# Gate and up as seven products of halves, positions in another order, joins by accumulating transfers, operands at multiples of 256 bytes

## The chip, the cores and the metric

The kernel runs on one core of one Trainium2 chip. The metric is the device time of one execution in microseconds (us). TensorE (PE; its weight loads are PEld), VectorE (DVE), ScalarE (ACT), GpSimd (POOL) and SyncE (SP) each work through their own instructions in order and wait for each other by semaphores. SyncE issues the transfers between main memory and the on-chip memory; a transfer that adds to its target is issued by GpSimd.

## What is computed

Position count S is 2,048, width D 640, hidden width F 1,536, 32 heads of 20 features. With x the input and xn its layer norm:

```python
qkv = xn @ wqkv                       # 640 -> 3 x 640
logits = q . k[i - 2w], w = 0..7      # each position sees itself and every second one before it
o = softmax(logits * scale) . v
s = o @ wo
h = (xn @ w_gate) * (xn @ w_up)       # 640 -> 1536, no nonlinearity
g = silu(h @ w_down)                  # 1536 -> 640
out = x + s * g
```

Since each position attends at distance 2, the even and the odd positions never meet: they are two independent rows.

## The kernel before, in words

All matrix products are done in three parts to keep float32's precision: each operand is split into hi (rounded to float32r, a ScalarE cast, L85) and lo (the rest, a subtraction, L86), and hi x hi, hi x lo and lo x hi are added in PSUM (`ALL3`, `mm3` at L95, `qkv` at L295).

The positions form 16 tiles of 128, `s` 0 to 7 even and 8 to 15 odd, in 4 chunks of 512 columns (`CH`). The even tiles are normalised and transposed on TensorE (`trans`, L229 to L231), the odd ones on VectorE (`trans_odd`, L209, L256, L259, L261); hi and lo of all four chunks then stay on chip in tiles `xc`.

Attention is split into 6 groups of heads (5 or 6 heads, 300 or 360 columns of q, k and v) and two halves of positions: 12 units (`UN`), ordered group by group, even then odd. For a unit TensorE does 8 x 15 products (`qkv`, L295), ScalarE takes q and k, v out of PSUM (L297, L298), a transfer shifts k and v by one partition (kv<-kv), and VectorE does the attention: 4 products with k (L329) each reduced (L332), the softmax (L336 to L345, with ScalarE's exponential at L341), 4 products with v (L350), 3 sums (L358) and a last one (L361). The result is stored in `o_scr`.

Between units TensorE does pieces of gate and up: for each of 12 blocks `f` of 128 hidden features and each of 4 chunks, 15 products of 512 columns for gate and 15 for up. ScalarE copies gate out (`gs`, L397), VectorE multiplies it by up (`hs`, L408; before the attention starts and after it ends, ScalarE and GpSimd do this at L410 and L411), and a transfer stores it in `h_scr` (L412). The weights of a block are loaded into `wraw`, cast by ScalarE and subtracted by GpSimd (`split_wf`).

The code is emitted in the order in which it shall run on each engine. VectorE's attention is a generator: `advance(budget)` gives it the TensorE time that has just been emitted, times `PACE`, as credit, and each of its steps costs an estimate in us; `finish_piece` places the multiplications, and `drain(u - 2)` ends a unit's attention before the unit after next begins. After the last block come the output projection (`out_proj`, tiles 0 to 15, 30 products of 320 columns each, L95; its operand is transposed by `trans_o`, L467, L85, L86), meanwhile the weights of down are summed and split, and at last down as seven products of halves for each pair of tiles (`product`, L606, 56 x 18 products), with silu (L587) and the gating (L592, L593).

The tiles' places in the on-chip memory follow from the order of their allocation. `xc` and `wf` begin at 128 or 96 bytes past a multiple of 256, and the qkv weights have rows of 1,200 or 1,440 bytes.

## Time and profile before

| | |
|---|---|
| runs shown | 787.12, 787.69, 788.05 us; median 787.69 |
| profiled execution, first to last instruction (span) | 786.0 us |
| around the span, by the median | 1.7 us |
| TensorE, VectorE, ScalarE, GpSimd busy | 778.0, 659.3, 234.2, 147.9 us |
| products on TensorE | 4,454 |
| moved by transfers | 92.7 MB, 118 GB/s in the mean |

All times within the profile count from the first instruction. "Busy" is the time in which an engine executes anything; a product's record reaches into the next one, so that the distance from product to product is read from a run of them (15 products in 3.50 us), not from a record. A line such as L95 is a line of the kernel before.

### The profile page before, as it was taken

The numbers are of one execution on the slowest core, as the hardware profiler recorded it, in microseconds if no ns is written. First come the engines' busy times: TensorE is split into PE (matmuls) and PEld (weight loads), VectorE is DVE, ScalarE is ACT, GpSimd is POOL, SyncE is SP. The second block draws the span as 40 slices with busy tenths as digits, with TensorE's granted clock in tenths as the row PEclk, the third lists the DMA queues.
The fourth block names the chain that finished last, engine by engine and source line by source line (L and its number), as shares of the span: only waits on it lengthen the run. The fifth ranks groups of instructions, "written<-read, shape, count | busy, mean of one in ns | idle before, by whom it ended". The sixth has DMA issues, their size and how long they took to land.

```text
span 786.0 us, 11222 instructions
## 1 busy us (share of the span) xinstructions
PE 778.0 (99%) x4454; PEld 708.9 (90%) x4454; DVE 659.3 (84%) x660; ACT 234.2 (30%) x536; POOL 147.9 (19%) x110
## 2 busy tenths in 40 slices
PE   8999999999999999999999999999999999999997
PEld 6889898888898898899898989888899999999997
DVE  6889899999999979996999999992177667777775
ACT  5334211121112111311221202012366564444442
POOL 5301211022013200410231000112467600000000
PEclk9999999999999999999999999999999999999999
DMA  8172122141132321404033131332797574555534
GB/s 321 67 230 75 42 61 72 48 123 48 50 83 89 95 71 61 117 28 112 28 105 86 58 86 58 107 103 66 160 274 209 170 270 131 206 200 188 182 101 135
DMA packets 81661, 92.68 MB, mean 118 GB/s; under 512 B 23032, under 2 KB 63304, under 8 KB 81480
## 3 DMA queue, kind: packets, MB, share of 16 engines
q1 hardware_dynamic: 81608, 91.96, 38.2%
q8 instruction: 35, 0.57, 0.3%
q14 instruction: 18, 0.15, 0.1%
HBM read 54.53 MB, written 28.31 MB: 105 GB/s over the span
## 4 chain that ended last, share of the span: by engine, by line
PE 97%; DMA 2%; ACT 1%; DVE 0%; SPq 0%; POOL 0%; issue 0%
PE q L295 26%; PE u L95 21%; PE g L95 21%; PE q L606 11%; PE q L95 9%; PE u L606 5%; PE g L606 3%; DMA wraw<-in_wgu 1%; DMA wraw<-in_wqkv 1%; PE q L229 0%; ACT wf L85 0%; SPq L135 0%; ACT wqh L85 0%; ACT xc L230 0%; POOL wql L86 0%; PE q L249 0%
## 5 line engine op out<-in xcount | busy, mean ns | idle before, releaser
L95 PE MATMUL u<-xc,wf 128*128 128x512 f32 (+1 forms) x735 | 176.2, 390 | 0.0
L95 PE MATMUL g<-xc,wf 128*128 128x512 f32 (+1 forms) x735 | 176.1, 390 | 0.0
L95 PEld LDWEIGHTS u<-xc,wf 128*128 128x128 f32 x735 | 135.7, 187 | 32.2
L95 PEld LDWEIGHTS g<-xc,wf 128*128 128x128 f32 x735 | 135.3, 187 | 31.0
L295 PE MATMUL q<-wqh,xc 128*128 128x300 f32 (+1 forms) x960 | 159.8, 309 | 2.1 <-DVE xc L231 1.2
L295 PEld LDWEIGHTS q<-wqh,xc 128*128 128x128 f32 x960 | 146.0, 188 | 4.3 <-DVE xc L231 1.5
L329 DVE TENSOR_TENSOR t<-q,kv 128x1600 f32<-128x1600 f32 (+1 forms) x48 | 97.9, 2040 | 10.1 <-DMA kv<-kv 10.1
L350 DVE TENSOR_TENSOR t<-e,kv 128x1600 f32<-128x1600 f32 (+1 forms) x48 | 97.5, 2051 | 1.1
L86 POOL TENSOR_TENSOR wf<-wraw,wf 128x256 fp32r<-128x256 f32 (+2 forms) x22 | 48.8, 2232 | 248.1 <-ACT wf L85 248.1
L332 DVE TENSOR_REDUCE lg<-t 128x80 f32<-128x1600 f32 (+1 forms) x48 | 92.6, 1930 | 1.2
L397 ACT ACTIVATE gs<-g 128x512 f32<-128x512 f32 x48 | 28.7, 598 | 205.9 <-PE g L95 197.2
L295 PE MATMUL q<-wql,xc 128*128 128x300 f32 (+1 forms) x480 | 86.3, 309 | 0.0
L358 DVE TENSOR_TENSOR t<-t,t 128x1600 f32<-128x1600 f32 (+1 forms) x36 | 80.2, 2228 | 1.1
L295 PEld LDWEIGHTS q<-wql,xc 128*128 128x128 f32 x480 | 74.4, 188 | 0.0
L297 ACT ACTIVATE kv<-q 128x200 f32<-128x200 f32 (+1 forms) x96 | 33.4, 348 | 129.4 <-PE q L295 129.4
L606 PE MATMUL q<-xc,wf 128*128 128x320 f32 x432 | 67.3, 309 | 0.0
L606 PEld LDWEIGHTS q<-xc,wf 128*128 128x128 f32 x432 | 64.3, 188 | 0.0
L86 POOL TENSOR_TENSOR wql<-wraw,wqh 128x300 fp32r<-128x300 f32 (+4 forms) x15 | 34.0, 2292 | 142.7 <-ACT wqh L85 142.7
L95 PE MATMUL q<-wf,wf 128*128 128x320 f32 x156 | 35.7, 310 | 0.0
L408 DVE TENSOR_TENSOR hs<-u,gs 128x512 f32<-128x512 f32 x39 | 26.6, 683 | 0.6 <-issue 0.6
L95 PEld LDWEIGHTS q<-wf,wf 128*128 128x128 f32 x156 | 26.1, 188 | 0.0
L86 DVE TENSOR_TENSOR wf<-ot,wf 128x640 fp32r<-128x640 f32 x13 | 15.5, 1190 | 11.9 <-ACT wf L85 11.9
(161 smaller groups left out, 888.9 us busy)
## 6 DMA issues: line engine op xcount, KB each, us to landing
h_scr<-hs SPq DMA_DIRECT2D x48, 256.0 KB, 2.3
wraw<-in_wgu SPq DMA_DIRECT2D x12, 640.0 KB, 4.9
t<-h_scr SPq DMA_DIRECT2D x8, 768.0 KB, 7.8
hs<-s_scr SPq DMA_DIRECT2D x16, 320.0 KB, 4.0
gs<-in_x SPq DMA_DIRECT2D x16, 320.0 KB, 4.4
wraw<-h_scr SPq DMA_DIRECT2D x12, 384.0 KB, 5.9
out<-q SPq DMA_DIRECT2D x14, 320.0 KB, 3.7
wraw<-in_wd SPq DMA_DIRECT2D x12, 320.0 KB, 4.8
```

Of the source, the lines that this page charges most:

```text
L86: eng.tensor_sub(lo, raw, hi.bitcast(F32))
L95: nc.tensor.matmul(acc, a, b, start=first and n == 0, stop=last and n == len(runs) - 1)
L295: nc.tensor.matmul(p, xT[(r * NE + i) // TPC][a][:, k, t0:t0 + P], wq[g][b][:, k], start=n == 0, stop=n == len(runs) - 1, skip_group_check ...
L297: nc.scalar.activation(kv_t[u][:, :, W - 1 + i, :], p[:, c:].rearrange("p (a c) -> p a c", a=2), AF.Copy)
L329: nc.vector.tensor_mul(t, q.rearrange("p i c -> p (i c)").unsqueeze(1).to_broadcast([P, 2, NE * c]), places(0, j))
L332: nc.vector.tensor_reduce(out=lg[:, :, j:j + 2].rearrange("p n a -> p a n"), in_=heads(t), op=ALU.add, axis=AX.X)
L350: nc.vector.tensor_mul(heads(t), pw, heads(places(1, j)))
L358: nc.vector.tensor_add(acc, acc, t)
L397: nc.scalar.activation(gs, pp[0], AF.Copy)
L408: nc.vector.tensor_mul(hs, pp[1], gs)
L606: nc.tensor.matmul(p, y[:, i, k], wd_t[name][k][:, l], start=new and r == 0, stop=r == len(runs) - 1, skip_group_check=True)
```

## The change

- **Seven products.** For 17 pairs of a block of hidden features and a half of the positions (`JOBS` of kind "S"), gate and up of both chunks are computed together: the two chunks are one side's halves, gate and up the other's, and the 640 contracted features are two halves of 256 and a rest of 128. Seven products on sums of weight blocks and sums of x blocks (`strassen`, L628) give the four results in 54 products of 512 columns; the rest of 128 is added into the same PSUM tiles. Seven other pairs (kind "P") stay as they were, 60 products. The last of the seven products of a job is deferred (`flush`) behind the first two of the next job or into the next unit.
- **Joins.** ScalarE copies the products out of PSUM, three accumulating transfers of 256 KB issued by GpSimd add them up (L656, L665, L669), and VectorE multiplies the joined results (L680).
- **Sums of weights and of x.** GpSimd forms four sums of each S block (L179 to L182), stored in `w_scr` and loaded again for the odd half. VectorE forms 9 sums of x for each half of the positions (L335 to L352), ScalarE and GpSimd split them.
- **Lo parts of weights.** Instead of a subtraction ScalarE writes the negative of hi into lo, and an accumulating transfer adds the weights from main memory (L154, L203 to L206).
- **Order.** All six groups of the even positions come first, then the six of the odd ones; the qkv weights are loaded for each unit, 12 times. Transposed tiles are stored in `xt_scr` (by way of the two buffers `ot`); hi and lo of the odd chunks are made later from it, and only one half's x stays on chip beside its sums. `ORDER` sets the sequence of jobs and units, `later` the emission of preparations some us of estimated TensorE time after their load, and `PACE` is 0.95.
- **Places.** Two unused tiles and padded rows put both operands of every large product at multiples of 256 bytes.

```diff
-PACE = 1.0
+PACE = 0.95
+MM = 0.2135
+GATE, UP = (0, 1, 2, 3, 6), (8, 9, 4, 5, 7)
+W_ROWS = ((0, 0), (1, 0), (2, 0), (3, 0), (2, 1), (3, 1), (4, 0), (4, 1), (0, 1), (1, 1))
...
+    ORDER = ("P", "S", "U", "S", "S", "U", "S", "S", "U", "S", "S", "U", "P", "P", "U", "P", "P", "U",
+             "S", "S", "U", "S", "S", "U", "S", "S", "U", "S", "S", "U", "S", "S")
+    JOBS = [(f, 0, "P" if f in (0, 1, 2, 10, 11) else "S") for f in range(KF)]
+    JOBS += [(f, 1, "P" if f in (10, 11) else "S") for f in (10, 11, 3, 4, 5, 6, 7, 8, 9, 0, 1, 2)]
+    FEED = {i: ((i + 2, 0),) for i in range(len(JOBS) - 2) if i not in (10, 11)}
+
+    def end_job(i):
+        for j, d in FEED.get(i, ()):
+            load_wf(j)
+        if i == len(JOBS) - 2:
+            load_wo(0)
+            load_wo(1)
+            later(7, lambda: (split_wo(0), split_wo(1)))
...
+    def later(us, act):
+        events.append((clock[0] + us, len(events), act))
+        events.sort(key=lambda e: e[:2])
+
+    def step(us):
+        clock[0] += us
+        while events and events[0][0] <= clock[0]:
+            events.pop(0)[2]()
+        advance(PACE * us)
...
+        cp = -(-c3 // 64) * 64
+        raw = st([P, KD, cp], "wql", 1)[:, :, :c3]
+        for k0, k1 in ((0, 3), (3, KD)):
+            nc.sync.dma_start(raw[:, k0:k1], wqkv[g][:, k0:k1])
+        later(7, lambda: split_wq(u, raw))
+
+    def split_wq(u, raw):
+        g = UN[u][0]
+        c3 = raw.shape[2]
+        cp = -(-c3 // 64) * 64
+        hi = st([P, KD, cp], "wqh", 1, F32R)[:, :, :c3]
+        ks = ((0, 2), (2, 4), (4, KD))
+        for k0, k1 in ks:
+            nc.scalar.activation(hi[:, k0:k1], raw[:, k0:k1], AF.Copy)
+        lo = st([P, KD, cp], "wql", 1, F32R)[:, :, :c3]
+        for k0, k1 in ks:
+            negate(hi[:, k0:k1], lo[:, k0:k1])
+        nc.gpsimd.dma_start(lo, wqkv[g], accum_op=ALU.add)
+        wq[u] = hi, lo
...
+    def wf_tile(dt=F32R):
+        return st([P, 16, P], "wf", 4, dt)
+
+    def load_wf(i):
+        f, r, kind = JOBS[i]
+        raw = wf_tile(F32)
+        if kind == "P":
+            nc.sync.dma_start(raw[:, :10], wgu[f])
+            later(6, lambda: split_wf(i, raw))
+        elif r and (f, 0, "S") in JOBS:
+            nc.sync.dma_start(raw[:, :8], wgu[f, :, :8])
+            nc.sync.dma_start(raw[:, 8:], w_scr[f])
+            later(7, lambda: split_wf(i, raw))
+        else:
+            nc.sync.dma_start(raw[:, :8], wgu[f, :, :8])
+            a21 = st([P, 2, P], "ot", 2)
+            nc.sync.dma_start(a21, wgu[f, :, 8:])
+            later(6, lambda: sum_wf(i, raw, a21))
+
+    def sum_wf(i, a, a21):
+        nc.gpsimd.tensor_add(a[:, 8:10], a21, a[:, 4:6])
+        nc.gpsimd.tensor_sub(a[:, 12:14], a[:, 0:2], a21)
+        nc.gpsimd.tensor_sub(a[:, 10:12], a[:, 8:10], a[:, 0:2])
+        nc.gpsimd.tensor_sub(a[:, 14:16], a[:, 2:4], a[:, 10:12])
+
+        def store():
+            nc.sync.dma_start(w_scr[JOBS[i][0]], a[:, 8:])
+            split_wf(i, a)
+
+        later(4, store)
...
+        def low():
+            lo = wf_tile()
+            for k0, k1 in cuts:
+                negate(hi[:, k0:k1], lo[:, k0:k1])
+            if kind == "P":
+                nc.gpsimd.dma_start(lo[:, :10], wgu[f], accum_op=ALU.add)
+            else:
+                nc.gpsimd.dma_start(lo[:, :8], wgu[f, :, :8], accum_op=ALU.add)
+                nc.gpsimd.dma_start(lo[:, 8:], w_scr[f], accum_op=ALU.add)
+            set_wf(i, hi, lo)
+
+        later(2.5, low)
...
+    st([P, 32], "skip", 1)
...
+    def store_xT(s, y):
+        c = (s % TPC) * P
+        nc.sync.dma_start(xt_scr[s // TPC, :, :, c:c + P], y)
...
+    def load_xS(r):
+
+        (ah, al), (bh, bl) = [[x_tile(1 - r), x_tile(1 - r)] for _ in range(2)]
+        a, b = xt_scr[2 * r], xt_scr[2 * r + 1]
+        xS[r] = {"T1": (ah, al, 0), "T2": (ah, al, 2), "T3": (bh, bl, 0), "T4": (bh, bl, 2), "D5": (ah, al, 4)}
+
+        def block(k):
+            ta, tb = st([P, 2, CH], "wraw", 3), st([P, 2, CH], "wraw", 3)
+            nc.sync.dma_start(ta, a[:, k:k + 3:2])
+            nc.sync.dma_start(tb, b[:, k:k + 3:2])
+
+            def sums():
+                nc.vector.tensor_sub(ta[:, 0], tb[:, 0], ta[:, 0])
+                nc.vector.tensor_sub(tb[:, 0], tb[:, 1], tb[:, 0])
+                nc.vector.tensor_sub(tb[:, 1], tb[:, 1], ta[:, 0])
+                nc.vector.tensor_sub(ta[:, 1], ta[:, 1], tb[:, 1])
+                credit[0] -= 2.4
+
+            later(8, sums)
+            for n, (t, hi, lo, j) in enumerate(((ta[:, 0], ah, al, k), (tb[:, 0], bh, bl, k),
+                                                (tb[:, 1], ah, al, k + 2), (ta[:, 1], bh, bl, k + 2))):
+                later(11 + 1.5 * n, lambda t=t, hi=hi, lo=lo, j=j: parts(nc.gpsimd, t, hi[:, j], lo[:, j]))
...
+            if k0 == 0:
+                full = st([P, KD, P], "ot", 2)
+            nc.scalar.activation(full[:, k0:k1], p, AF.Copy)
...
+        store_xT(s, full)
...
-        hi, lo = xT_tile(s)
-        nc.scalar.activation(hi, y, AF.Copy)
-        low_parts()
-        halves.append(lambda: nc.vector.tensor_sub(lo, y, hi.bitcast(F32)))
...
+        store_xT(s, y)
...
+    st([P, 24], "gap", 1)
...
-            if running:
-                nc.vector.tensor_mul(hs, pp[1], gs)
-            else:
-                nc.scalar.activation(hs, pp[1], AF.Copy)
-                nc.gpsimd.tensor_mul(hs, hs, gs)
-            nc.sync.dma_start(h_scr[ch * TPC:(ch + 1) * TPC, :, f, :].rearrange("t p c -> p t c"),
-                              hs.rearrange("p (t c) -> p t c", c=P))
+            nc.vector.tensor_mul(hs, pp[1], gs)
+            credit[0] -= 0.7
+            store_h(ch, JOBS[i][0], hs)
 
...
+    def strassen(i):
+        f, r, _ = JOBS[i]
+        x = lambda name: xs(r, name)
+        A, C, B = pt([P, CH], "g", 2), pt([P, CH], "u", 2), pt([P, CH], "u", 2)
+        m, v = st([P, 2, CH], "wraw", 3), st([P, 2, CH], "wraw", 3)
+        t = prod(A, i, [((0, 1), x("B11"))], True)
+        copy(m[:, 0], A)
+        step(t)
+        t = prod(C, i, [((8, 9), x("T1"))], True)
+        copy(m[:, 1], C)
+        finish_piece()
+        step(t)
+        flush()
+        t = prod(B, i, [((2, 3), x("B21")), ((6,), x("A5"))], True)
+        ha = copy(st([P, CH], "hs", 2), B)
+        nc.gpsimd.dma_start(ha, m[:, 0], accum_op=ALU.add)
+        finish_piece(1)
+        step(t)
+        t = prod(A, i, [((10, 11), x("T2"))])
+        copy(v[:, 0], A)
+        finish_piece()
+        step(t)
+        t = prod(C, i, [((14, 15), x("B22")), ((6,), x("B5"))])
+        hb = copy(st([P, CH], "gs", 2), C)
+        nc.gpsimd.dma_start(hb, v[:, 0], accum_op=ALU.add)
+        step(t)
+        t = prod(A, i, [((12, 13), x("T3")), ((7,), x("B5"))])
+        copy(v[:, 1], A)
+        nc.gpsimd.dma_start(v[:, 1], m[:, 1], accum_op=ALU.add)
+        step(t)
+
+        def last():
+            t = prod(A, i, [((4, 5), x("T4")), ((7,), x("D5"))])
+            unfinished.append(lambda: finish(2 * r + 1, hb, v[:, 1]))
+            unfinished.append(lambda: finish(2 * r, ha, A))
+            step(t)
+            end_job(i)
+
+        def finish(ch, y, z):
+            nc.vector.tensor_mul(y, y, z)
+            credit[0] -= 0.7
+            store_h(ch, f, y)
+
+        deferred.append(last)
...
     qkv(0, 5)
     moments(12, 2, mvo[:, 4:6])
     moments(14, 2, mvo[:, 6:8])
-    load_xq(12, 3, xa)
-    load_xq(15, 1, xd)
+    load_xq(12, 4, xc[2])
     nc.vector.tensor_copy(mro[:, 0, :], mvo[:, :, 0])
     rstd(mvo[:, :, 1], mro[:, 1, :], NE)
+    qkv(0, 6)
+    qkv(0, 7)
+    load_wq(1)
     gate_up(0, 1, amid=(spread,))
-    trans_odd(8)
...
-        if i == 2:
-            load_wq(1, ((0, 3), (3, 5)))
-            low_parts()
         if i < 2:
             trans_odd(14 + i)
+        if i == 2:
+            load_xS(0)
         qkv(1, i)
...
         for i in range(NE):
-            if u % 2 and u + 1 < len(UN) and i == 2:
-                load_wq(UN[u + 1][0], ((0, 3), (3, 5)))
             qkv(u, i)
-            if i == 1:
-                finish_piece()
-            advance(PACE * GROUPS[UN[u][0]] * 0.38)
+            if i == 0:
+                flush()
+            if i in (1, 2):
+                finish_piece(1)
+            step(15 * (0.138 if GROUPS[UN[u][0]] == 5 else 0.16))
+        if u + 1 < len(UN):
+            load_wq(u + 1)
         running.append((u, attention(u)))
...
+    at = 2
+    u = 2
+    for what in ORDER:
+        if what == "U":
+            unit(u)
+            if UN[u] == (len(GROUPS) - 1, 0):
+                load_xT(2)
+                later(12, lambda: load_xT(3))
+            if UN[u] == (0, 1):
+                load_xS(1)
+            if u == len(UN) - 1:
+                load_wo(2)
+                load_wo(3)
+                later(8, lambda: (split_wo(2), split_wo(3)))
+            u += 1
+            continue
+        i = at
+        at += 1
+        if JOBS[i][2] == "P":
+            flush()
+            for ch in range(2):
+                gate_up(i, 2 * JOBS[i][1] + ch)
+            end_job(i)
+        else:
+            strassen(i)
+    load_wo(KD - 1)
+    load_o(0, 1, st([P, 1, D], "ot", 2))
+    flush()
+    advance(1e9)
+    finish_piece()
+    step(100)
+    split_wo(KD - 1)
+    load_wd(0)
+    trans_o(0)
+    load_o(1, 1, st([P, 1, D], "o", 1))
+    load_o(2, 3, st([P, 3, D], "t", 2))
+    load_o(5, 3, st([P, 3, D], "t", 2))
```

Three places in the order. First TensorE, between one S job and the next. Before, a block with its first two chunks (g and u are the PSUM tiles of gate and up, wf the weights, hi and then lo):

```order
L95 MATMUL g_1290<-xc_134,wf_1072 128x512 x10
L95 MATMUL g_1290<-xc_134,wf_1073 128x512 x5
L95 MATMUL u_1291<-xc_134,wf_1072 128x512 x10
L95 MATMUL u_1291<-xc_134,wf_1073 128x512 x5
L95 MATMUL g_1332<-xc_424,wf_1072 128x512 x10
L95 MATMUL g_1332<-xc_424,wf_1073 128x512 x5
L95 MATMUL u_1333<-xc_424,wf_1072 128x512 x10
L95 MATMUL u_1333<-xc_424,wf_1073 128x512 x5
```

After, the second S job after a unit begins (weights wf_1354 and wf_1398), with the deferred last product of the job ahead (PSUM tile g_1431) behind its second:

```order
L628 MATMUL g_1514<-xa_138,wf_1354 128x512 x2
L628 MATMUL g_1514<-xa_139,wf_1354 128x512 x2
L628 MATMUL g_1514<-xa_138,wf_1398 128x512 x2
L628 MATMUL u_1515<-xb_858,wf_1354 128x512 x2
L628 MATMUL u_1515<-xb_859,wf_1354 128x512 x2
L628 MATMUL u_1515<-xb_858,wf_1398 128x512 x2
L628 MATMUL g_1431<-xb_860,wf_1255 128x512 x2
L628 MATMUL g_1431<-xb_858,wf_1255 128x512
L628 MATMUL g_1431<-xb_861,wf_1255 128x512 x2
L628 MATMUL g_1431<-xb_859,wf_1255 128x512
L628 MATMUL g_1431<-xb_860,wf_1301 128x512 x2
L628 MATMUL g_1431<-xb_858,wf_1301 128x512
```

Each row of 512 columns now stands in runs of two or three with a copy out of PSUM between, and a PSUM tile is added to again after its copy.

Second GpSimd, at the same place. Before, the lo subtractions of the qkv weights (wql) and of the blocks' weights (wf):

```order
L86 TENSOR_TENSOR wql_939<-wraw_811,wqh_938 128x900
L86 TENSOR_TENSOR wql_939<-wraw_813,wqh_938 128x600
L86 TENSOR_TENSOR wf_1073<-wraw_522,wf_1072 128x1280
L86 TENSOR_TENSOR wf_1352<-wraw_1288,wf_1351 128x1280
L86 TENSOR_TENSOR wql_1639<-wraw_1508,wqh_1638 128x900
L86 TENSOR_TENSOR wql_1639<-wraw_1510,wqh_1638 128x600
```

After, the sums of a block (wf_1250), two accumulating loads of its lo (wf_1398), the joins of the job ahead (hs, gs, wraw) with the next unit's qkv lo (wql) between them:

```order
L179 TENSOR_TENSOR wf_1250<-ot_1252,wf_1250 128x256
L180 TENSOR_TENSOR wf_1250<-wf_1250,ot_1252 128x256
L181 TENSOR_TENSOR wf_1250<-wf_1250 128x256
L182 TENSOR_TENSOR wf_1250<-wf_1250 128x256
L205 DMA wf_1398<-in_wgu 128x1024
L206 DMA wf_1398<-w_scr 128x1024
L656 DMA hs_1467<-wraw_1434 128x512
L665 DMA gs_1490<-wraw_1435 128x512
L154 DMA wql_1497<-in_wqkv 128x5x300
L669 DMA wraw_1435<-wraw_1434 128x512
```

The subtractions are gone, and the joins stand in one order with the preparation of weights.

Third VectorE at the end of attention. Before, the last steps of the last unit and the first output tile (ot is the transposed tile):

```order
L408 TENSOR_TENSOR hs_4401<-u_4343,gs_4359 128x512
L358 TENSOR_TENSOR t_4288<-t_4288,t_4289 128x1920
L361 TENSOR_TENSOR o_4405<-t_4288 128x960
L467 STREAM_TRANSPOSE ot_4564<-wraw_4301 128x640
L86 TENSOR_TENSOR kv_4566<-ot_4564,kv_4566 128x640
L467 STREAM_TRANSPOSE ot_4625<-o_4569 128x640
```

After, the same with the last job's joined tiles (gs, hs) ahead of the first output tile:

```order
L541 TENSOR_TENSOR t_5095<-e_4990,kv_798 128x1920
L549 TENSOR_TENSOR t_5094<-t_5094,t_5095 128x1920
L552 TENSOR_TENSOR o_5103<-t_5094 128x960
L680 TENSOR_TENSOR gs_5041<-gs_5041,wraw_4970 128x512
L680 TENSOR_TENSOR hs_5017<-hs_5017,g_4966 128x512
L713 STREAM_TRANSPOSE ot_5115<-ot_5066 128x640
L89 TENSOR_TENSOR kv_5117<-ot_5115,kv_5117 128x640
L713 STREAM_TRANSPOSE ot_5138<-o_5120 128x640
```

The rows of attention are the same; what moved is TensorE's work beside them, which before still had blocks of gate and up here.

304 lines of the change are left out of this document (162 added, 142 removed).

## The prediction

> **What bounds the kernel now.** I read busy time by engine first, then the chain that ended last, then the stages.
>
> ```profile
> PE 778.0 (99%) x4454; PEld 708.9 (90%) x4454; DVE 659.3 (84%) x660; ACT 234.2 (30%) x536; POOL 147.9 (19%) x110
> ```
>
> TensorE is busy throughout. The chain in order of time (start us, us, what) shows the pace of its products and the stages:
>
> ```profile
> 28.16 1.09 PE q L229 x10
> ...
> 269.10 16.48 PE q L295 x120
> 285.58 3.50 PE g L95 x15
> ...
> 344.05 19.84 PE q L295 x120
> ...
> 563.36 70.60 PE q L95 x480
> 633.96 2.64 PE q L606 x18
> ...
> 779.10 2.65 PE q L606 x18
> ...
> 782.76 0.49 DVE q L593
> ```
>
> Gate, up and qkv end at 563.4, the output projection takes 70.6, down 147.8, the tail 4.2: a span of 786.0. The median of the runs shown is 787.69, 1.7 above the span; I add that at the end. A product takes 3.50/15 = 233 ns on 512 columns, 137 on 300, 165 on 360, 147 on 320: always 0.456 to 0.460 ns per column, so columns are the cost and nothing per product. The same stages by engine (busy us and count of PE, PEld, DVE, ACT, POOL, then the granted clock, DMA share, GB/s):
>
> ```profile
> 60.50:563.40 502.90, 502.90 (x2642) 442.24 (x2642) 451.03 (x323) 103.44 (x268) 87.08 (x33) 1.00 0.27 76
> 563.40:634.00 70.60, 70.60 (x482) 70.60 (x481) 45.65 (x56) 38.74 (x90) 42.79 (x43) 1.00 0.76 211
> 634.00:786.00 152.00, 147.73 (x1008) 147.47 (x1006) 115.50 (x147) 68.06 (x113) 0.00 (x0) 1.00 0.52 179
> ```
>
> VectorE is close behind in the first (451 of 503), not in the others. The clock is granted in full, so no throttle slows the products.
>
> **Part 1, products removed.** Two chunks of gate and up are 60 products. The seven products contract 2, 2, 3, 2, 3, 3 and 3 blocks, 18 in all, times three hi/lo parts: 54. There are 17 such jobs, so 17 x 6 = 102 products of 233 ns go: **-23.8 us of TensorE**, whose gate-and-up end would move from 563.4 to 539.6.
>
> **Part 2, operand starts.** No product of this trace has both operands at a multiple of 256 bytes, so the price must be bounded. Upper end: nothing changes, 0.456 to 0.460 per column. Lower end, from the transposes in the chain above, which hold plain float32 and not the rounded kind of all other products: 1.09/10/128 = 0.852 per column. If these are two steps for each column, a step is 0.426, and the rounded products take 1.07 to 1.08 steps, as if their operands arrived late. I take **0.426**: an array that works in whole steps, held up by its reads, is the reading that explains the odd 1.08. Against it: a unit's rows of qkv weights start at many remainders of 256, zero among them, and 120 products still take an even 16.48; but there the other operand never starts at a multiple.
>
> The Trainium skill's "TensorE: Matmul & The Clock Gate", section "Back-to-back issue gap", gives a warm isolated gap of N/2.4 + 2.5 ns, that is 215.8 for 512 columns and 135.8 for 320. The trace's 233 and 147 disagree with it; with the page's figure the last two stages would give back 16.4 us instead of the 15.7 below.
>
> At 0.426, 512 columns take 218 ns, 360 take 153, 320 take 136.3, 300 take 128. In gate, up and qkv that is 1,308 x 15 + 480 x 12 + 960 x 9 = 34 us more, so TensorE by itself could end there at about 505. In the last two stages, where TensorE sets the end: 480 x (147.1 - 136.3) + 1,008 x (146.7 - 136.3) = **-15.7 us**.
>
> **Part 3, what is late next: VectorE.** Its lines from 70 to 535 us (busy us, mean ns, idle before, releaser):
>
> ```profile
> L329 DVE TENSOR_TENSOR t<-q,kv 128x1600 f32<-128x1600 f32 (+1 forms) x48 | 97.9, 2040 | 10.1 <-DMA kv<-kv 10.1
> L350 DVE TENSOR_TENSOR t<-e,kv 128x1600 f32<-128x1600 f32 (+1 forms) x48 | 97.5, 2051 | 1.1
> ...
> L358 DVE TENSOR_TENSOR t<-t,t 128x1600 f32<-128x1600 f32 (+1 forms) x36 | 80.2, 2228 | 1.1
> L408 DVE TENSOR_TENSOR hs<-u,gs 128x512 f32<-128x512 f32 x39 | 26.6, 683 | 0.6 <-issue 0.6
> L361 DVE TENSOR_TENSOR o<-t 128x800 f32<-128x800 f32 (+1 forms) x12 | 18.4, 1534 | 0.3
> ...
> L343 DVE TENSOR_REDUCE sm<-e 128x40 f32<-128x320 f32 (+1 forms) x12 | 6.1, 508 | 8.3 <-ACT e L341 8.3
> ```
>
> and its order of time at the first odd tile, at attention's start, at one meeting with GpSimd and at attention's end (GpSimd's own row follows):
>
> ```profile
> 46.33 1.18 DVE L209 TENSOR_SCALAR xc<-xc,mrq 128x160 f32<-128x160 f32 x4 [2.04 <-DMA xc<-in_xq]
> 47.55 0.85 DVE L256 STREAM_TRANSPOSE ot<-xc 128x640 f32<-128x640 f32 x1
> ```
> ```profile
> 69.85 1.82 DVE L329 TENSOR_TENSOR t<-q,kv 128x1600 f32<-128x1600 f32 x1
> ```
> ```profile
> 99.25 4.49 DVE L358 TENSOR_TENSOR t<-t,t 128x1600 f32<-128x1600 f32 x1
> ```
> ```profile
> 528.78 2.16 DVE L350 TENSOR_TENSOR t<-e,kv 128x1920 f32<-128x1920 f32 x1
> ...
> 533.64 1.16 DVE L361 TENSOR_TENSOR o<-t 128x960 f32<-128x960 f32 x1
> ```
> ```profile
> 98.19 3.86 POOL L86 TENSOR_TENSOR wf<-wraw,wf 128x1280 fp32r<-128x1280 f32 x1 [14.30 <-ACT wf L85]
> ```
>
> Transfers and single operations that the terms need (KB each, median us to landing; busy, mean ns):
>
> ```profile
> h_scr<-hs SPq DMA_DIRECT2D x48, 256.0 KB, 2.3
> wraw<-in_wgu SPq DMA_DIRECT2D x12, 640.0 KB, 4.9
> ...
> s_scr<-gs SPq DMA_DIRECT2D x10, 320.0 KB, 3.2
> ...
> o_scr<-o SPq DMA_DIRECT2D x2, 480.0 KB, 3.1
> ...
> o<-o_scr SPq DMA_DIRECT2D x4, 80.0 KB, 4.4
> ```
> ```profile
> L397 ACT ACTIVATE gs<-g 128x512 f32<-128x512 f32 x48 | 28.7, 598 | 205.9 <-PE g L95 197.2 <-issue 5.2 <-POOL wqh L86 1.7
> ...
> L86 DVE TENSOR_TENSOR wf<-ot,wf 128x640 fp32r<-128x640 f32 x13 | 15.5, 1190 | 11.9 <-ACT wf L85 11.9
> ...
> L467 DVE STREAM_TRANSPOSE ot<-t 128x640 f32<-128x640 f32 x14 | 11.7, 834 | 1.9 <-DMA t<-o_scr 1.9
> ...
> L85 ACT ACTIVATE wf<-ot 128x640 fp32r<-128x640 f32 x13 | 9.6, 735 | 9.7 <-DVE ot L467 9.7
> ...
> L86 POOL TENSOR_TENSOR wf<-wraw,wf 128x256 fp32r<-128x256 f32 x10 | 7.0, 731 | 3.0 <-ACT wf L85 3.0
> ```
>
> Attention takes VectorE 534.8 - 69.85 = 465.0 us. After the change:
> - Start. Two more qkv positions (4.1 us) come ahead of the odd means, less 1.4 by faster products: the odd tiles begin at 49. Each costs 1.18 + 0.85 = 2.0 on VectorE, but its buffer (there are two) must be stored before reuse; with 3.2 to land 320 KB and 0.4 between, a tile takes (2.0 + 3.2 + 0.4)/2 = 2.8. Eight, the last two unhindered, 20.8, and 1.1 for multiplications that ScalarE and GpSimd used to do: **70.9**. Bounds: 66 with the stores hidden, 74 with no faster products and slower stores. On SyncE the same stores stand ahead of the loads of x for the sums.
> - Length: 465.0, less the 10.1 for which L329 waited for TensorE's newest kv; 5 multiplications more here, x 0.683 = 3.4; 18 sums of blocks of x, x 0.683 (nearest row L408) = 12.3.
> - GpSimd. The operation that met its subtraction took 4.49 instead of 1.82: 2.67 for 1,280 elements, 2.1 ns each. Before, 20,900 elements run there, 44 us if every one met; L329, L350, L358 and L361 together took 294.0 against 267.6 at the undisturbed 1.82 and 2.16, so 26 were lost. After, the weights' lo subtractions leave, but 40 sums of 256 and 28 subtractions of 512 come: 24,576 elements, 51 us if all met, 31 at the same share: +4.6. Bounds -26 to +25.
> - ScalarE gets 68 more product copies of 0.6, the negations, twice as many casts of qkv weights and 28 casts of x; its share here goes from 103 of 503 to about a half. Attention waits for it at L343; I take half of those 8.3 again, +4.2; bounds 0 and 17.
>
> Sum: 70.9 + 465.0 - 10.1 + 3.4 + 12.3 + 4.6 + 4.2 = **550.3**, where TensorE, at 505 to 540, must wait.
>
> Preparing weights I cost at nothing: a job's weights are loaded two jobs ahead, with a job of 54 x 0.218 = 11.8 us and mostly a unit of qkv (16.5) between, against a load of 4.9, four sums of 0.73, eight ScalarE passes of 0.6 and two accumulating loads of 4.9 each, some 22 us. Without that cover TensorE would stand still for what is missing.
>
> **Part 4, the seam.** The first eight output tiles need even positions alone, but their transposes stand behind the last attention operation on VectorE. From 550.3: 0.83 (transpose) + 0.74 (cast) + 1.19 (lo) = 2.8 to the first product. The second tile's load waits for the last store: 3.1 + 4.4 + 2.8 = 10.3, while the first tile is done at 2.8 + 30 x 0.136 = 6.9: 3.4 more. So the projection effectively starts at 556.5 instead of 563.4: **-6.9**. Sum: 786.0 - 6.9 - 15.7 = 763.4, plus 1.7: **765.1 us**.
>
> **The rivals.**
> - *Operand starts give nothing.* For it the even 16.48; against it the 1.08 steps. VectorE still sets 556.5, the last stages keep their time: 765.1 + 15.7 = **780.8**.
> - *The joins come late* (slower). Each job adds three results by accumulating transfers, and VectorE multiplies the joined tiles at a fixed place of its order: if one is not there, the attention behind it waits too. Between the copy that starts the last join and that multiplication lie 30 products, 6.5 us, against 0.6 for the copy and 2.3 for 256 KB by the nearest row. But GpSimd issues two 512 KB accumulating loads of weights ahead of the joins; with one of 4.9 in front it is 7.8, with two 12.7. Half of that lateness, 3 us, in 17 jobs is 51: **816**. It decides from (787.7 - 765.1)/17 = 1.3 us per job. No accumulating transfer runs in this trace, so nothing speaks directly for or against it.
> - *GpSimd no longer slows VectorE*, its shorter operations falling beside reductions: 31 us less, **734**, with TensorE just behind.
>
> On the joins, the Trainium skill's "SBUF — State Buffer", section "A bandwidth-pool intuition that's wrong (but worth ruling out)", says that a transfer issued by GpSimd can wait for VectorE, 620 ns becoming 3,100 beside a copy. No run here shows it; by that figure each join would land some 2.5 us later.
>
> **How the numbers follow.** Forecast 0.50 (765), operand starts without gain 0.22 (781), late joins 0.18 (816), VectorE freed 0.10 (734). The range 738 to 792 takes in the start's bounds (-5, +3), GpSimd's -26 and ScalarE's +13, the second case with 11 us more, and joins late by 1.5 us. Within 0.2% (1.6 us), about what a measurement of this kernel can tell from no change: 0.04, where errors cancel. Slower 0.19: the joins and a little of the second case. Faster 0.77.
>
> **What would show it.** Part 2: 15 products on 512 columns in 3.27 against 3.50, 18 on 320 in 2.45 against 2.64. Part 3: attention ending near 550 and TensorE standing still, most of all just before the projection. Joins: VectorE idle ahead of the multiplication of joined tiles, released by a DMA. I am wrong altogether if TensorE waits for weights.

## The result, and the profile after

The changed kernel takes **934.91 us** (median of 4 runs, 929.07 to 936.5) against 787.87 for the kernel before on the same chip: a ratio of 1.185, 95% interval 1.181 to 1.189. The forecast was 765.1. The profiled execution has a span of 934.2 us, 170.8 more than the 763.4 that the prediction's sum gave for the span. One run of an experiment (`e16_no_lo_gate_up`), in which the granted clock was 0.82 against 0.94 in the other, is left out of the times below.

First the busy time by engine, and what the transfers did (packets, MB, share of the time of 16 transfer engines):

```profile
PE 785.2 (84%) x4352; PEld 712.1 (76%) x4352; DVE 681.9 (73%) x679; ACT 377.7 (40%) x831; POOL 256.6 (27%) x252
...
q1 hardware_dynamic: 106808, 124.54, 42.5%
q0 software_dynamic: 19888, 42.23, 26.4%
```

No engine is busy throughout any more: TensorE fell from 99% to 84%, VectorE from 84% to 73%. Queue q0 is GpSimd's, with all accumulating transfers; the kernel before had nothing on it. Its 42 MB cost 26.4% where 125 MB of ordinary transfers cost 42.5%: 1.8 times as much per byte.

The stages, as in the table of before (busy us of PE, PEld, DVE, ACT, POOL, granted clock, transfer share, GB/s):

```profile
92.40:702.20 609.80, 492.96 (x2466) 428.06 (x2464) 465.81 (x326) 238.47 (x534) 194.18 (x173) 0.91 0.73 171
702.20:782.10 79.90, 73.75 (x481) 73.48 (x482) 47.80 (x60) 38.76 (x90) 42.24 (x42) 0.95 0.75 206
782.10:934.20 152.10, 147.86 (x1009) 147.60 (x1007) 115.66 (x147) 67.83 (x113) 0.00 (x0) 1.00 0.50 179
```

The first row runs from VectorE's first attention operation to its last. It took 609.8 us where 479.4 were forecast, yet VectorE was busy for 465.8 of it, close to the forecast's work. So 144 us are waiting. What VectorE waited for from 60 to 712 us (the row of L449 lies ahead of attention), then TensorE and ScalarE from 20 to 712 us (us in total, times, longest):

```profile
DVE gs L680 <- DMA wraw<-wraw: 73.3, 8, 13.9
DVE sm L534 <- ACT e L532: 44.9, 12, 9.4
DVE ot L449 <- DMA xt_scr<-ot: 13.3, 4, 6.9
DVE gs L680 <- DMA wf<-w_scr: 12.2, 1, 12.2
DVE wraw L335 <- DMA wraw<-xt_scr: 7.1, 3, 4.3
```
```profile
PE g L628 <- ACT wraw L638: 58.8, 17, 8.6
PE q L129 <- ACT kv L88: 34.5, 1, 34.5
PE q L486 <- DMA wql<-in_wqkv: 14.7, 2, 10.3
```
```profile
ACT wqh L150 <- DMA wql<-in_wqkv: 38.4, 10, 9.1
ACT wraw L638 <- DMA wraw<-wraw: 38.1, 7, 8.0
...
ACT wf L92 <- DMA w_scr<-wf: 25.9, 6, 8.7
```

L680 is the multiplication of joined tiles: 85.5 us of waiting for the joins (the one wait put down to `wf<-w_scr` ended at the landing of a join, too). L534 waits for ScalarE's exponential, 44.9 us against 8.3 before. ScalarE itself stood before loads, joins and the stores of weight sums. TensorE's largest wait but one is the 34.5 us before the projection, for the end of attention.

One join in order of time (start us, us, engine, line, operation; in brackets the idle time before it and what ended it):

```profile
499.25 1.34 POOL L154 DMA_DIRECT2D wql<-in_wqkv  x1 [2.48 <-ACT wql L92]
...
500.11 1.39 POOL L669 DMA_DIRECT2D wraw<-wraw  x1
...
511.46 0.69 DVE L680 TENSOR_TENSOR gs<-gs,wraw 128x512 f32<-128x512 f32 x1 [9.59 <-DMA wraw<-wraw]
511.48 0.60 ACT L638 ACTIVATE wraw<-g 128x512 f32<-128x512 f32 x1 [7.11 <-DMA wraw<-wraw]
...
512.13 1.22 PE L628 MATMUL g<-xa,wf 128*128 128x512 f32 x2 [4.99 <-ACT wraw L638]
```

GpSimd issues 750 KB of weights and right behind them the last join of a job. The join is there 11.3 us later. VectorE has then stood for 9.6 us before the multiplication; ScalarE for 7.1 before a copy into a tile that the join still read; and TensorE for 5.0, since it may not add to a PSUM bank before ScalarE has copied it. One late transfer stops three engines. The transfers of that line and their time to landing:

```profile
DMA to landing us min/median/max: 3.2/7.2/12.1
```

This case is typical. Seven of the 17 last joins were issued 0.9 us behind a load of qkv weights and landed 9.0 to 12.1 us later, and at these seven landings end the seven longest waits of L680 (6.4 to 13.9 us, 82 of the 85.5). By the start and landing times in the trace, 26 of all 51 joins were issued while a load of weights was still under way in GpSimd's queue. Each of them landed after that load, 4.5 to 12.1 us after its own start (median 8.3). The other 25 took 3.2 to 7.4 us (median 3.4).

### The profile page after: what moved, and what is told of

Read it like the earlier page. It is cut to its first block, busy times and chain, and to the rows that moved or that the text cites. A ratio compares the mean times of both kernels' runs of the same rounds, so it can differ in the third digit from the quotient of the medians.

```text
span 934.2 us, 11836 instructions
## 1 busy us (share of the span) xinstructions
PE 785.2 (84%) x4352; PEld 712.1 (76%) x4352; DVE 681.9 (73%) x679; ACT 377.7 (40%) x831; POOL 256.6 (27%) x252
## 3 DMA queue, kind: packets, MB, share of 16 engines
q1 hardware_dynamic: 106808, 124.54, 42.5%
q0 software_dynamic: 19888, 42.23, 26.4%
## 4 chain that ended last, share of the span: by engine, by line
PE 44%; DMA 23%; DVE 14%; issue 7%; POOL 5%; ACT 4%; SPq 2%; POOLq 0%; ACTq 0%; DVEq 0%
PE q L486 12%; PE q L853 9%; DMA wraw<-wraw 9%; PE q L129 7%; DMA wql<-in_wqkv 6%; PE g L628 5%; PE u L853 5%; DVE t L541 4%; DMA w_scr<-wf 4%; DVE t L549 3%; PE g L853 2%; DVE t L520 2%; PE u L628 2%; DMA xt_scr<-ot 2%; DVE lg L523 2%
## 5 line engine op out<-in xcount | busy, mean ns | idle before, releaser
L628 PE MATMUL g<-xb,wf 128*128 128x512 f32 x237 | 75.8, 439 | 33.7 <-ACT wraw L638 33.7
L628 PE MATMUL g<-xa,wf 128*128 128x512 f32 x273 | 81.9, 420 | 25.2 <-ACT wraw L638 25.2
L486 PE MATMUL q<-wqh,xa 128*128 128x300 f32 (+1 forms) x480 | 83.7, 318 | 9.4 <-DVE xa L424 7.8
L628 PEld LDWEIGHTS g<-xb,wf 128*128 128x128 f32 x237 | 49.9, 215 | 47.6 <-ACT wraw L638 37.2
L628 PEld LDWEIGHTS g<-xa,wf 128*128 128x128 f32 x273 | 54.1, 203 | 40.2 <-ACT wraw L638 29.2
L486 PEld LDWEIGHTS q<-wqh,xa 128*128 128x128 f32 x480 | 75.9, 196 | 11.3 <-DVE xa L424 8.1
L486 PE MATMUL q<-wqh,xb 128*128 128x300 f32 (+1 forms) x480 | 81.3, 313 | 0.0
L486 PEld LDWEIGHTS q<-wqh,xb 128*128 128x128 f32 x480 | 75.2, 194 | 1.1
L628 PE MATMUL u<-xb,wf 128*128 128x512 f32 x222 | 58.8, 405 | 19.5 <-DMA wf<-w_scr 6.5
L680 DVE TENSOR_TENSOR gs<-gs,wraw 128x512 f32<-128x512 f32 x17 | 12.8, 755 | 85.5 <-DMA wraw<-wraw 73.3
L628 PEld LDWEIGHTS u<-xb,wf 128*128 128x128 f32 x222 | 42.5, 194 | 31.5 <-ACT xb L304 6.9
L628 PE MATMUL u<-xa,wf 128*128 128x512 f32 x186 | 52.1, 426 | 1.9 <-DVE hs L601 1.8
L486 PE MATMUL q<-wql,xa 128*128 128x300 f32 (+1 forms) x240 | 45.0, 319 | 10.3 <-DMA wql<-in_wqkv 10.3
L92 ACT ACTIVATE wf<-wf 128x512 fp32r<-128x512 f32 (+1 forms) x77 | 41.7, 617 | 29.1 <-DMA w_scr<-wf 25.9
L154 POOL DMA_DIRECT2D wql<-in_wqkv x11 | 15.0, 1368 | 135.2 <-ACT wql L92 120.4
L196 ACT ACTIVATE wf<-wf 128x512 fp32r<-128x512 f32 (+1 forms) x77 | 42.6, 620 | 18.5 <-DMA w_scr<-wf 6.7
```

The costliest lines, as they stand in the source:

```text
L92: nc.scalar.activation(lo, hi.bitcast(F32), AF.Copy, scale=-1.0)
L196: nc.scalar.activation(hi[:, k0:k1], raw[:, k0:k1], AF.Copy)
L486: nc.tensor.matmul(p, xT[(r * NE + i) // TPC][a][:, k, t0:t0 + P], wq[u][b][:, k], start=n == 0, stop=n == len(runs) - 1, skip_group_check ...
L628: nc.tensor.matmul(p, y, x, start=first and n == 0, stop=n == len(runs) - 1, skip_group_check=True)
```

## The experiments

Three questions: is it the joins or the weights; what is the rest; and what are operand starts worth? All times are medians beside the kernel before (787.3 to 787.9) on the same chip. The accumulating loads of weights are 48 in the trace (17 + 17 + 3 for gate and up, 11 for qkv); the expectations count 45 and 34 in places.

**Without joins** (`e1_no_joins`):

```diff
-        nc.gpsimd.dma_start(ha, m[:, 0], accum_op=ALU.add)
...
-        nc.gpsimd.dma_start(hb, v[:, 0], accum_op=ALU.add)
...
-        nc.gpsimd.dma_start(v[:, 1], m[:, 1], accum_op=ALU.add)
```

> Left out: the three accumulating transfers that join the results of a seven-product job (51 in all), so the gate and up values of those chunks are incomplete. Theory J (the joins land late and hold up VectorE, ScalarE and TensorE in turn): VectorE's 85.5 us of waits ahead of its multiplications of joined tiles go, and most of its 44.9 us of waits for the exponential with them, since ScalarE no longer stands before a copy whose tile a join still uses: 935 - 85 - 35 = about 815. Theory W (the weights themselves come late, and the joins only wait beside them): TensorE and VectorE wait as long for weights instead, 890 or more.

Measured: 883.96 us (880.0 and 887.9). Between the two: the joins are worth 51 us, not 120. VectorE's waits for the exponential did not go with them, as the first theory has it; they rose from 44.9 to 69.4 us:

```profile
DVE sm L534 <- ACT e L532: 69.4, 12, 13.5
```

**Without the accumulating loads of low parts** (`e2_no_lo`), the joins kept:

```diff
-        nc.gpsimd.dma_start(lo, wqkv[g], accum_op=ALU.add)
...
-            if kind == "P":
-                nc.gpsimd.dma_start(lo[:, :10], wgu[f], accum_op=ALU.add)
-            else:
-                nc.gpsimd.dma_start(lo[:, :8], wgu[f, :, :8], accum_op=ALU.add)
-                nc.gpsimd.dma_start(lo[:, 8:], w_scr[f], accum_op=ALU.add)
```

> Left out: the 45 accumulating loads that turn the negated high parts of gate, up and qkv weights into low parts, so those products use a wrong low part. The joins stay and have GpSimd's queue to themselves. Theory J, with the queue as its cause (a join is late because 512 to 900 KB of weights stand ahead of it): each join lands in some 3.2 us, the shortest of the run after, and the waits for joined tiles fall from 85 us to under 15: 830 or less. Theory J without the queue (an accumulating transfer is slow in itself): joins still land in about 7 us and the time stays above 900. Theory W: about as fast as the first case, but then the run without joins stays slow.

Measured: 839.62 us, 95 less. The same joins now land in (last join of a job, then VectorE's wait for it):

```profile
DMA to landing us min/median/max: 3.2/3.7/7.2
```
```profile
DVE gs L674 <- DMA wraw<-wraw: 20.4, 11, 3.6
```

3.7 us instead of 7.2 in the median, and a wait of 20 instead of 73 in the row of that name. An accumulating transfer is not slow in itself; it was late behind the weights.

**Without both** (`e5_no_joins_no_lo`):

> Left out: both the joins and the accumulating loads of the weights' low parts. If the joins cost only because the weights stand ahead of them in the queue, then without the weights they were nearly free (VectorE still waited 20 us for them), and this run is at 815 to 825, some 20 under the run without low parts. If joins and weights are two separate losses, they add: 935 - 51 - 95 = 789.

Measured: 836.02 us, a little above the first case's 815 to 825: with the queue empty the joins cost 3.6 us. The four runs make a table of two by two:

| | joins | no joins | joins cost |
|---|---|---|---|
| with loads of low parts | 934.9 | 884.0 | 51 |
| without | 839.6 | 836.0 | 3.6 |
| the loads cost | 95 | 48 | |

So of the 147 us some 47 come only where the two meet, 48 are the loads of low parts alone, 4 the joins alone, and 48 are neither; with 8 us between the two runs without joins, these parts are good to some 4 us. That the two meet in GpSimd's queue, and not only in the transfer engines, is seen in the landing times above: no join overtook a load. These runs do not show by which path the loads alone cost 48.

**Which loads.** The 11 of qkv left out alone (`e15_no_lo_qkv`, the first line of the diff of `e2_no_lo`), then those of gate and up alone (`e16_no_lo_gate_up`, its other lines):

> The kernel after; left out are only the 11 accumulating loads of the low parts of the qkv weights (8.9 MB); the 34 of gate and up (17.4 MB) and the 51 joins stay. If what counts is how much stands in GpSimd's queue ahead of joins, a third of the 95 us that all of them cost: about 903. If the single buffer of the qkv weights is the trouble (load, cast, negation and accumulation of one unit's weights stand in a row between two units): 60 us or more of it, 875 or less.

> The kernel after; left out are only the 37 accumulating loads of the low parts of the gate and up weights; the 11 of qkv and the 51 joins stay. By the amount in the queue: two thirds of the 95 us, about 872. If the qkv weights are the trouble: 900 or more.

Measured: 883.0 without those of qkv (-52) and 889.5 without those of gate and up (-45; a single run). Neither expectation held: the qkv loads, half the bytes, cost as much as the others, and the two add up to the 95. Amount alone does not order them, and the single buffer of qkv weights is not the whole trouble either. With the qkv loads gone VectorE's waits were

```profile
DVE sm L533 <- ACT e L531: 44.8, 12, 8.7
DVE gs L679 <- DMA wraw<-wraw: 43.7, 12, 6.8
```

that is 30 of the 73 us for the joins had gone, those for the exponential had not. The trace of the kernel after shows a part of why the qkv loads weigh more than their bytes. They stand directly ahead of a job's last join, at whose landing VectorE goes on; the loads of gate and up stand ahead of the first two, for which no engine is seen to wait.

**Joins on VectorE** (`e6_joins_on_vector`), with nothing of the result left out. The diff shows the three joins; VectorE makes each together with multiplications of the job before it or later:

```diff
-        nc.gpsimd.dma_start(ha, m[:, 0], accum_op=ALU.add)
+        unfinished.append(lambda: join(ha, m[:, 0]))
...
-        nc.gpsimd.dma_start(hb, v[:, 0], accum_op=ALU.add)
+        unfinished.append(lambda: join(hb, v[:, 0]))
...
-        nc.gpsimd.dma_start(v[:, 1], m[:, 1], accum_op=ALU.add)
+        finish_piece()
+        unfinished.append(lambda: join(v[:, 1], m[:, 1]))
...
+    def join(y, z):
+        nc.vector.tensor_add(y, y, z)
+        credit[0] -= 0.7
```

> The 51 joins are made by VectorE, an addition of 512 elements each at the place where the multiplications of the job before are made, instead of accumulating transfers; the low parts of the weights stay accumulating loads. Nothing of the result is left out. VectorE gets 51 x 0.69 = 35 us more and loses its 85 us of waits for joined tiles. If the late joins are worth what their absence showed (51 us), and the additions cost their own time on the engine that sets the end: 884 + 35 = 919. If the additions fall into the waits that are left (105 us of idle VectorE without joins): 884 to 895.

Measured: 916.08 us, the first case. VectorE's busy time within attention rose from 466 to 498 us, its idle time fell from 143 to 92.

**All jobs plain** (`e3_all_plain`; the loads of x for its sums, `load_xS`, are left out with them), then the same without the loads of low parts (`e10_plain_no_lo`):

```diff
-    JOBS = [(f, 0, "P" if f in (0, 1, 2, 10, 11) else "S") for f in range(KF)]
-    JOBS += [(f, 1, "P" if f in (10, 11) else "S") for f in (10, 11, 3, 4, 5, 6, 7, 8, 9, 0, 1, 2)]
+    JOBS = [(f, 0, "P") for f in range(KF)]
+    JOBS += [(f, 1, "P") for f in (10, 11, 3, 4, 5, 6, 7, 8, 9, 0, 1, 2)]
```

> All 24 jobs plain, 60 products each: no seven products, no joins, no sums of weights or of x; the accumulating loads of low parts and the operand starts stay. Nothing of the result is left out. Theory J: without joins the weight loads have cover, and 102 products more cost 23 us of TensorE; it stays near TensorE's own sum, 785 to 800. Theory W (the accumulating loads and the long preparation are the loss): 850 or more.

> All 24 jobs plain and, left out, all accumulating loads of low parts, so that no accumulating transfer is left in the kernel. It splits the 48 us that stay above the kernel before (836 against 788) with joins and low parts both left out. If they come with the seven products (sums of weights and of x, their splits, more copies): 790 to 800, TensorE's own sum. If they come with the rest of the change (weights of gate and up loaded and cast twice, those of qkv too, high part and negation both on ScalarE): 820 to 835, as all plain with low parts was at 824.

Measured: 824.08 and 808.78 us. The first lies between its two theories. The loads of low parts cost 15 us here, not 48 as with seven products, where a job loads 1,024 KB of them instead of 640. The second lies between its theories too: of the 48 us that are neither joins nor low parts, 27 go with the seven products (although these save 102 products) and 21 stay without them. For the 27 compare the traces of `e10_plain_no_lo` and `e5_no_joins_no_lo`: with seven products attention starts 6 us later (84.3 against 78.4) and lasts 20 us longer (519.1 against 499.1), and VectorE is busy in it for 448 us instead of 419. In the plain kernel GpSimd was busy for 37 us of attention, against 71 before. The four rows of VectorE that the prediction compared, 294.0 us before and 267.6 undisturbed, took 268.9 there, so 25 of the 26 us that it gave to meetings with GpSimd went with GpSimd's work. But attention lasted 499 us, and the last operation of the last unit stands far behind that unit's last qkv product. First the kernel before (a row of TensorE and one of VectorE; the end of attention, 534.8, is in the prediction), then `e10_plain_no_lo`:

```profile
485.38 0.99 PE L295 MATMUL q<-wqh,xc 128*128 128x360 f32 x5
490.73 2.15 DVE L329 TENSOR_TENSOR t<-q,kv 128x1920 f32<-128x1920 f32 x1
```
```profile
529.48 0.96 PE L480 MATMUL q<-wqh,xb 128*128 128x360 f32 x5
535.73 2.16 DVE L514 TENSOR_TENSOR t<-q,kv 128x1920 f32<-128x1920 f32 x1 [6.82 <-DMA kv<-kv]
576.38 1.16 DVE L546 TENSOR_TENSOR o<-t 128x960 f32<-128x960 f32 x1
```
```profile
PE q L129 <- ACT kv L88: 22.1, 1, 22.1
```

The last attention ends some 47 us after the last qkv product, in both kernels (576.38 + 1.16 against 529.48 + 0.96; 534.8 against 486.4). Before, 330 products of 512 columns came behind the last unit, 77 us, and covered it. In the new order 120 come (108 with seven products), 27 us, and TensorE stands still for 22.

**More attention per product time.** `PACE` from 0.95 to 1.06, in the plain kernel without low parts (`e11_plain_no_lo_pace`) and in the kernel after (`e12_after_pace`):

> All jobs plain and no accumulating loads, as in the run at 809 (low parts left out), with the planner's share of attention raised from 0.95 to 1.06: a product is planned at 0.2135 us and takes 0.227, so 0.95 hands VectorE only 0.89 us of attention for each us of TensorE, and 1.06 hands it 1.0. Theory P (the plan itself leaves VectorE idle and attention over at the end): VectorE's 79 us of idle time within attention fall to 30 to 50, TensorE's 22 us of standing still before the projection go, 785 to 795. Rival (VectorE's idle time comes from ScalarE's casts and from transfers, whatever the plan): 805 to 812.

> The kernel after with the same share, 1.06 instead of 0.95, and nothing else changed. Theory P would take from it what it takes from the plain kernel, and VectorE would come later to the joined tiles and wait less for them: 900 to 915. If late weights and joins alone make the loss, attention that is handed out earlier only waits at other places: 930 to 940. If VectorE then comes too late to the multiplications that free TensorE's banks: above 940.

Measured: 808.19 and 939.64 us: nothing won in the one, and 5 us lost in the other. The plan's share was not the cause by itself. With more of it the waits only moved: in `e11_plain_no_lo_pace` those for the exponential fell from 42.7 to 7.4 us, and VectorE ran out of units earlier and waited for the keys and values:

```profile
DVE sm L528 <- ACT e L526: 7.4, 9, 1.7
DVE t L514 <- DMA kv<-kv: 55.9, 7, 12.9
```

**The last units earlier** (`e13_plain_no_lo_order`), then with both edits (`e17_plain_order_pace`):

```diff
-             "S", "S", "U", "S", "S", "U", "S", "S", "U", "S", "S", "U", "S", "S")
+             "S", "S", "U", "S", "U", "S", "S", "U", "S", "U", "S", "S", "S", "S")
```

> All jobs plain, accumulating loads left out (so low parts are wrong), and the table of the order changed so that four jobs instead of two follow the last unit; two of the earlier pairs of jobs become single jobs. Theory O (attention of the last unit, some 47 us, cannot begin before that unit's keys and values are there, and the change left only 120 products of 0.227 us = 27 us of TensorE behind it, where 330 products stood before): the last unit ends 27 us earlier, its attention ends before the products do, TensorE no longer stands still before the projection (22 us): 785 to 790. Rival (VectorE is simply short of time in this version, wherever the units stand): attention ends where it did, 577, and the time stays at 805 to 810.

> All jobs plain, accumulating loads left out (low parts wrong), with both edits that were tried one by one: four jobs behind the last unit, and the planner's share at 1.06. If the two limits hide each other (with the old order VectorE runs out of units, with the old share it comes late to the last one), together they give more than the 0.6 and 11 us of each alone: attention ends before the products do, near 550, and the time is 784 to 789. If VectorE is held by something else, the time stays at 797.

Measured: 797.56 and 793.09 us. The place of the last unit gave 11.2 us, less than the 20 expected; with the share it gave 15.7 of the 21. So the order is most of that part and hid the share. The 5.6 that remain were not followed up; attention starts 11 us later there than before (80.9 against 69.9). The new order was not run with seven products.

**Operand starts.** The kernel after with all tiles moved by 128 bytes (`e4_shifted`), the kernel before with the stationary operand moved from 96 to 128 past a multiple of 256 (`e7_before_filler`), and with all operands at such multiples (`e8_before_all_256`). In order, one piece from each kernel:

```diff
-    st([P, 32], "skip", 1)
...
+    st([P, 8], "gap", 1)
...
+    st([P, 32], "skip", 1)
...
+                st([P, 24], "gap", 1)
+            wq[g] = [st([P, KD, -(-c3 // 64) * 64], tag, 1, F32R)[:, :, :c3] for tag in ("wqh", "wql")]
```

> The kernel after without its 128-byte filler tile, so that all later tiles, the operands of the products among them, start 128 bytes past a multiple of 256. If the operand starts make the products faster, 512 columns go back from 227 to 233 ns and 360 columns from 160 to 165, while 320 stay at 147, as they did in the change. If something else made the 512 columns faster, they stay at 227 and 160. The time stays within 1% of 935 either way, as TensorE is not what bounds it.

> The kernel before with 32 bytes of filler ahead of the weight tiles, so that the stationary operand of gate, up, output projection and down starts at 128 instead of 96 past a multiple of 256; nothing else is changed. If the start of the stationary operand makes the 512-column products of the change faster: 1,410 x (233.5 - 227) ns = 9.2 us less, 778, with 320 columns still at 147. If not: 787 to 788.

> The kernel before with every operand of the large products at a multiple of 256 bytes, rows of qkv weights included; nothing else is changed. If operand starts are the cause of the faster products in the change: 512 columns at 227 and 360 at 160, so 9.2 + 480 x 5 ns = 11.6 us less, 776. If not: 787 to 788. By the prediction's step of 0.426 us per 1,000 columns it would be some 50 us less on TensorE.

Measured: 935.76; 789.65 (ten runs from 781.8 to 792.3; ratio 0.9999, 0.9969 to 1.0029); 789.96 (ten runs from 785.3 to 792.5; 1.0027, 1.0008 to 1.0045). The products did become faster, the kernel before did not. In `e7_before_filler` 15 products of 512 columns take 3.42 us, 18 of 320 columns 2.64 as before, and TensorE now waits for the multiplication that frees its bank:

```profile
29.96 3.42 PE g L95 x15
...
638.33 2.64 PE q L607 x18
```
```profile
PE u L95 <- DVE hs L409: 6.7, 4, 2.3
```

In the shifted kernel after, 512 columns stayed at 227 ns: a multiple of 128 is as good as one of 256.

**The same, with the plan told of it** (`e9_before_256_pace`):

```diff
-PACE = 1.0
+PACE = 0.975
```

> The kernel before with all operands at multiples of 256 bytes, as in the run ahead of it, and the planner's share of attention per product time lowered from 1.0 to 0.975, the ratio of the new to the old product (227 / 233). If the faster products gained nothing because VectorE, given attention by the old product time, now comes late to the multiplications that free TensorE's banks, those waits go and the gain of 11.6 us is seen: 776 to 779. If VectorE's attention has become the bound itself, it ends as much later as it was thinned out, the waits only move to the projection, and the time stays at 787 to 790.

Measured: **776.94 us**, ratio 0.9862 (0.9846 to 0.9878), with nothing of the result left out: the best version here, 1.4% faster than the kernel before. Its wait for VectorE and its projection:

```profile
PE u L95 <- DVE hs L411: 1.3, 2, 0.7
```
```profile
552.22 70.39 PE q L95 x480
```

The projection starts at 552.2 instead of 563.4. VectorE had been given attention by the old product time; told of the new one, it comes in time to free the banks. By the distances between product starts, TensorE stood still for 11.0 us ahead of the projection in `e8_before_all_256` and lost 5.0 to products farther apart than usual; here it is 4.3 and 1.6. The lower share was not run with the old starts, but there TensorE was busy throughout that stage and had no such wait to lose.

## Why the prediction was wrong, step by step

The gap of 170.8 us on the span by the prediction's own terms (forecast, measured from the rows above and from the first and the last row of attention):

```profile
92.49 1.81 DVE L520 TENSOR_TENSOR t<-q,kv 128x1600 f32<-128x1600 f32 x1
...
700.58 1.16 DVE L552 TENSOR_TENSOR o<-t 128x960 f32<-128x960 f32 x1
```

| term | forecast | measured | gap |
|---|---|---|---|
| start of attention | 70.9 | 92.5 | 21.6 |
| length of attention | 479.4 | 609.2 | 129.8 |
| from its end to down, less 480 products | 6.2 | 9.7 | 3.5 |
| 480 products of the projection | 65.4 | 70.6 | 5.2 |
| down and tail | 141.5 | 152.2 | 10.7 |

1. *102 products fewer.* They are gone, but TensorE set no end. By the distances between product starts up to the projection, some 520 us are products at their usual pace, some 150 standing still, and 30 are lost by products farther apart than usual.
2. *Operand starts, "I take 0.426"*: wrong. 512 columns went to 227 ns (0.443 per column) and 360 to 160; 320 stayed at 147 and 300 at 137, so the last two stages gave none of the 15.7 us. The even 16.48 that stood against it was a true sign, for 300 columns take some 137 ns at any start; the step of 0.426 came from transposes alone, and no other product came to it. By the Trainium skill's "TensorE: Matmul & The Clock Gate", section "Back-to-back issue gap", an isolated product of 512 columns takes 215.8 and one of 320 takes 135.8 ns; no run came to either.
3. *VectorE the bound.* Its busy time was right: 440.2 before and 3.4 + 12.3 + 4.6 more make 460.5, and 466 were measured (for the 4.6, the four rows beside GpSimd took 296.1 us, 2.1 more than before). Its idle time was not: 24.7 before, less 10.1 and 4.2 more, make 19 against 143. This is the step that failed: the sum has no term for the joins, and counts the preparation of weights (point 4) as nothing. The rival on the joins had the mechanism, "VectorE idle ahead of the multiplication of joined tiles, released by a DMA", and weights ahead of the joins in GpSimd's queue, but a chance of 0.18. It named the loads of gate and up. What stood right ahead of the last join in seven jobs was the larger load of qkv weights, as the listing of GpSimd's order under the change has it, and the rival asked only how long VectorE stands, not ScalarE and TensorE. That its price, 51 us, is what leaving out the joins gave is luck: it took 3 us in each of 17 jobs, where seven waits of 6.4 to 13.9 us were measured, and without the loads the joins cost 3.6.

   The term for ScalarE, "+4.2; bounds 0 and 17", measured 44.9 - 8.3 = 37: half its share busy was taken for half the wait, when what counts is what stands ahead of the exponential in ScalarE's order. In the trace that is, of the 44.9 us, some 14 for splitting weights, 16 for copies of q, k and v and for the qkv products that they wait for, 9 for the store of weight sums and 5 for the exponential itself; no wait for a join is among it. Nor do accumulating transfers make it: it is 42.7 us in `e10_plain_no_lo`, which has none, and 7.4 there with a share of 1.06.
4. *"Preparing weights I cost at nothing"*: the largest single error. The loads of low parts cost 48 us without any join and 95 with them. Some 22 us of preparation were set against 28 of cover (11.8 and 16.5), without asking what else stands in the same queues. TensorE did wait for weights: 14.7 us in the row of L486. The start of attention is part of it: 92.5, and 82.5 without these loads; the other 12 us beyond the forecast's 70.9 were not explained.
5. *The seam* was near (9.7 against 6.2), but the sum took attention as a length of VectorE's work from its start. It left out that a unit's attention cannot begin before its qkv products, and that the order left 108 products behind the last unit, as `ORDER` in the diff shows.

The range ended at 792, above it lay 0.18 for the joins at 816. That rival had weights ahead of the joins, but took half of the lateness; no case had weights that come late themselves.

On the joins the prediction cited the Trainium skill's "SBUF — State Buffer", section "A bandwidth-pool intuition that's wrong (but worth ruling out)", by which a transfer from GpSimd can wait for VectorE. The runs did not need it: beside a VectorE that was busy for 86% of attention, the joins landed in 3.3 to 3.8 us (median by line) once the weights were gone.

What stays open: the rest of why the qkv loads cost as much as those of gate and up with twice the bytes (without them VectorE still waited 43.7 us for joins), and how the 48 us of the loads alone, 15 in the plain kernel, divide between GpSimd's queue, ScalarE's and the transfer engines.

## What to carry to other kernels

Price a new transfer by what is ahead of it in its queue and by who stands still until it lands, not by a lone transfer of its size; joins that cost 3.6 us by themselves cost 51 here behind loads of weights. When work is moved ahead of a dependent chain, check what is left to cover the last link: 27 us behind a unit that needs 47 made TensorE wait, whatever was saved in products. And a faster engine gives nothing until the plan that paces its neighbours is told: the same 11 us of product time were worth nothing at a share of 1.0 and 11 us at 0.975.

## What the runs showed of the hardware

- *Start of the stationary operand.* At 96 bytes past a multiple of 256 a product of 512 columns takes 233.5 ns, at 128 or 0 it takes 227; with 320 columns it is 147 at each (kernels before and after, `e4_shifted`, `e7_before_filler`). Of 360 columns, moving rows at odd starts take 165 ns, at multiples of 128 bytes 160; of 300 columns, 137 to 138 at both.
- *The clock after a stall.* Up to the stall at 507 us products of 512 columns came every 227 ns. After 5.0 us without work they came every 427 ns until 516. Three stretches (before, just after, and then): the granted clock is the third number from the end of each row.

```profile
500.00:506.90 6.90, 6.90 (x32) 5.56 (x30) 1.83 (x2) 0.86 (x2) 2.36 (x3) 1.00 0.89 168
512.20:516.00 3.80, 3.80 (x9) 3.06 (x10) 3.77 (x4) 0.37 (x1) 0.86 (x1) 0.50 0.69 157
516.00:520.00 4.00, 4.00 (x24) 3.60 (x24) 3.97 (x3) 3.12 (x8) 0.86 (x1) 0.96 1.03 218
```

  Products more than 1.08 but less than 2.3 times their usual distance apart lost some 30 us in sum before the projection, beside some 150 us of standing still: a stall is paid again in the products behind it. The Trainium skill's "TensorE: Matmul & The Clock Gate", section "Back-to-back issue gap", gives N / 1.2 ns for N columns on a cold array, 426.7 for 512; the trace agrees with 427.
- *Accumulating transfers.* 256 KB within SBUF land in 3.2 us at best. None of the 26 that were issued behind an unfinished load of the same queue landed before it.
